# One piece a slot: moving the third batch's first DFT forward, and giving the first expert block its own two PSUM banks

## The chip, the cores and the metric

The program runs on one core of one Trainium2 chip. The metric is device time in microseconds (us), the median of 3 runs. Engines are named as in the profile: PE (TensorE matmuls), PEld (its weight loads), DVE (VectorE), ACT (ScalarE), POOL (GpSimd), SP (SyncE, which issues most DMAs); SPq and ACTq are the DMA-issuing instructions of SP and ACT.

## The reference

`x` has 8 batches of 2496 tokens with 256 features. Step one filters every feature along the tokens in the frequency domain, step two is a mixture of 8 experts with two chosen per token:

```python
X = np.fft.rfft(x, axis=1)
y = np.fft.irfft(X * (filt_r + 1j * filt_i)[None], n=2496, axis=1)
logits = y @ w_gate;  noise_scale = np.log1p(np.exp(y @ w_noise))
top2 = the two largest of logits + noise_scale * noise;  top2_w = softmax over the two
for e in range(8):
    h = np.maximum(y[mask_e] @ w1[e], 0.0)          # 256 -> 1024
    out[mask_e] += top2_w * (h @ w2[e])             # 1024 -> 256
```

## The kernel before

**The filter.** A length of 2496 is 39 x 64. Per batch, 11 pieces of `x` (each 128x512, 256 KB) go through a first DFT of length 39 (`s1`, two-pass fp32 matmul at L338, copy to SBUF by ACT at L381, stored to a scratch tensor `fd` by SP at L382). `kgl` reloads them, `kg1` (L410) does the length-64 DFT and multiplies by the filter (ACT L427 and L428, DVE L429 and L430, POOL L431), `kg2` (L449) the inverse. `logit_sum` (L462), `logits` and `gating` (lg, L491 to L493) give the gate values; `t3` (transposes, L510, ACT L515) and `i2` (L532, ACT L542) end the inverse and write the rows `y` (SP L552). `gate` and `slots` (DVE, with rk at L934, sl at L1005, st at L1030) and `route` (L1072, ra; transposed at L1079) make the list of tokens of each expert, written by POOL (L1091).

**The experts.** A block is 512 token places of one expert. SP reads its list (`lt`, L1109), POOL gathers the rows (L1165). A block of the first batch is turned by POOL (L1237) and PE (xps, L1245); later blocks are turned by DMA transposes (L1204). Weights come by SP (L1291) and are split into two parts by ACT (L1329) and DVE (L1330). The first layer is 8 groups of 6 matmuls (hps, each 128x512; results drained by ACT L1378 and DVE L1379), the second 96 matmuls (yps, each 128x256; drained by ACT L1407, added to `out` by POOL L1408). Two blocks can be filled from the first batch alone; the third needs the list of the second batch.

**The order.** Before the first block, `fft_stream` follows a table: `at(slot, f, ...)` puts a step into a slot, and slots 0 to 31 are issued in order. Batch one runs from slot 0, batch two from slot 14 (its `kg1` in slots 14 to 23, `logit_sum` in slot 26); the third batch's `s1` was put into slots 26 to 31. `pin` makes every engine, SP included, keep the order as written for these steps. The experts, gating and routing are placed between them by the scheduler, from its own estimate of when inputs are ready; the order it settles on is fixed for the chip, and each engine executes its own list strictly in that order. `zero_out` clears rows of `out` (SP L311).

**Banks.** PSUM has 8 banks: hps 2, yps 2, xps 1, fps 3. In the early part `s1` uses the hps banks, and in slots 26 to 31 `t3` and `i2` use the yps banks. A first layer takes hps, hps and a third bank in turn: one of yps for blocks of the first batch (`third`, L1360).

Of the kernel before, what the change touches and what calls it, by code (L numbers as in the profile page):

```python
# [122 lines left out]
def _mm3(nc, o, lh, ll, rh, rl, start=True, stop=True):  # L123
    nc.tensor.matmul(o, lh, rh, start=start, stop=False)  # L124
    nc.tensor.matmul(o, lh, rl, start=False, stop=False)  # L125
    nc.tensor.matmul(o, ll, rh, start=False, stop=stop)  # L126


def f32v(ap):
    return ap.bitcast(F32)  # L130
# [22 lines left out]
class Moe:  # L153
    def __init__(self, ctx, tc, io):
        self.tc, self.nc, self.io = tc, tc.nc, io
        nc = self.nc
        self.cp = ctx.enter_context(tc.tile_pool(name="cp", bufs=1))
        self.dp = ctx.enter_context(tc.tile_pool(name="dp", bufs=1, space=DRAM))
        self.y = self.dp.tile([NROW, YW], I32, name="y")
        self.lst = self.dp.tile([NLR, LR], F32, name="lst")  # L160
        self.wpl = self.dp.tile([E, 2, 4, 128, 1024], F16, name="wpl")
        self.P = ctx.enter_context(tc.tile_pool(name="P", bufs=1))
        self.PS = ctx.enter_context(tc.tile_pool(name="PS", bufs=1, space=PSUM))
        self.xx, self.early, self.last = {}, True, {}
        self.writes, self.reads = [], []
        self.held = self.held_any = False
        self.banks = dict(EARLY)
        self.setup()
        self.tabs, self.wodd = [], 0
        self.sp = self.spw = self.lasta = None  # L170

    def after(self, i):
        return self.tc.issue_after(i.ins) if i is not None else nullcontext()
# [505 lines left out]
    def fft_stream(self):  # L679
# [7 lines left out]
        todo = [(bt, g) for bt in range(NB) for g in range(0, NG, 2)]  # L687
# [33 lines left out]
        def at(slot, g, *a):  # L721
            plan.setdefault(slot, []).append(f(g, *a))
# [22 lines left out]
        at(0, self.load_more)  # L745
        at(0, ahead, 19)
        at(8, self.setup2)
        at(20, ahead, 30)

        for j in range(11):  # L750
            at(7 + j // 2, s1, 11 + j)
# [10 lines left out]
                    at(o, self.t3, *R[i + 1])  # L762
                at(o, self.i2, *R[i])
        for j in range(11):
            at(26 + j // 2, s1, 22 + j)
        at(1, self.init_dram)
        for i in range(4):
            at(18 + i, self.zero_out, 0, i)
            at(24 + i, self.zero_out, 1, i)

        self.pin(self.load_first)
        for j in range(11):
# [568 lines left out]
    def expert(self, parts, may, fill=None):  # L1341

        nc, P = self.nc, self.P
        self.parts, self.ahead, self.standing, self.early_l = parts, [], 0, None
        self.fetch(lambda: True)
        cur = None
        while self.ahead:
            if cur is None:
                cur = self.front(self.ahead[0], fill)
            ent = self.ahead.pop(0)  # L1350
            blk, i = ent[:2]
            lt, n, nt, s, tabi, ready = blk
            w = 128 * nt
            w1, xT, w2st, sc = cur
            if i == 0:
                w2, adds = [], []
            ids, gate = lt[:, i], xT[2]
            if not self.ahead or self.ahead[0][3] or sum(len(a[2][0]) for a in self.ahead) < 4:
                self.fetch(may)
            third = ("xps", 1) if self.by_dma(ent) else ("yps", 2)  # L1360
            hh = []
            for f in range(8):

                tag, bufs = ("hps", 2) if f % 3 < 2 else third
                p = self.PS.tile([128, 512], F32, name="hps", tag=tag, bufs=bufs)[:, :w]
                for kc in range(2):
                    wh, wl = w1[f // 2]
                    o = (f % 2) * 128
                    _mm3(nc, p, wh[:, kc, o:o + 128], wl[:, kc, o:o + 128], *xT[kc], start=(kc == 0), stop=(kc == 1))
                h = P.tile([128, 512], R32, name="hh", bufs=8)  # L1370
                l = P.tile([128, 512], R32, name="hl", bufs=8)
                if ready >= HALF:
                    h, l = hf = h.bitcast(F16)[:, :w], l.bitcast(F16)[:, :w]
                else:
                    h, l = h[:, :w], l[:, :w]
                    hf = f32v(h),
                hold = lambda g: self.pin(g) if self.rows == NB - 1 else g()
                self.relu = hold(lambda: nc.scalar.activation(h, p, AF.Relu))  # L1378
                v = hold(lambda: nc.vector.scalar_tensor_tensor(l, p, 0.0, hf[0], op0=ALU.max, op1=ALU.subtract))  # L1379
                self.resid = v  # L1380
                if f == 4:
                    self.early_l = v
                hh.append((h, l))
                q = (f if f < 4 else None) if n == 1 and nt == 4 else f // 2 if f % 2 else None
                if q is not None and i == 0:
                    w2.append(self.wsplit(w2st[q], "w2", sc))
                yield
            late = not self.ahead
            if late:
                self.fetch(lambda: True)  # L1390
            if self.ahead:
                e2 = self.ahead[0]
                cur = (w1, self.turn(e2), None, sc) if e2[1] else self.front(e2, fill if late else None)
            self.fetch(may)
            yield
            for t in range(nt):


                if t % 2 == 0:
                    bank = self.PS.tile([128, 2, D], F32, name="yps", bufs=2)  # L1400
                p = bank[:, t % 2]
                for f in range(8):
                    h, l = (a[:, t * 128:(t + 1) * 128] for a in hh[f])
                    hl = w2[f // 2][:, :, f % 2]
                    _mm3(nc, p, h, l, hl[:, 0], hl[:, 1], start=(f == 0), stop=(f == 7))
                o = self.slot("yo")
                nc.scalar.activation(o, p, AF.Copy, scale=gate[:, t])  # L1407
                a = nc.gpsimd.indirect_dma_start(  # L1408
                    out=self.io["out"][:BLK + ready * ROWS], out_offset=bass.IndirectOffsetOnAxis(ap=ids[:, t:t + 1], axis=0),
                    in_=o, in_offset=None, compute_op=ALU.add)  # L1410
                for q in adds:
                    self.tc.declare_no_dep(a.ins, q.ins, reason="distinct rows of one expert")
                adds.append(a)
                self.lasta = a
                yield
# [120 lines left out]
```

## Time and profile before

| | us |
|---|---|
| median of 3 runs (2159.06 to 2162.99) | 2160.69 |
| the profiled execution's own time | 2158.89 |
| its span, first to last instruction | 2157.1 |
| PE busy in the span | 2094.6 (97%) |
| DVE, ACT, POOL busy | 1465.0, 1286.0, 1029.5 |
| mean granted TensorE clock, of full speed | 0.993 |

The profiled execution lies 1.80 us under the median. PE is busy nearly throughout, so what can move the end is mostly the time in which PE stands idle, 62.5 us in all.

### The profile page before, as it was taken

To read this page: it belongs to the slowest core of one execution; us is meant where nothing else is said; L and a number is where in the kernel's file an instruction comes from. 1 tells how busy PE (TensorE), PEld (TensorE's weight loads), DVE (VectorE), ACT (ScalarE), POOL (GpSimd) and SP (SyncE) were. 2 spreads that over 40 slices of the span, in tenths; PEclk is the share of its full clock that TensorE was granted. 3 is DMA by queue.
4 is the path that set the end of the run, shared out by engine and by line. 5 is a ranking of instruction groups with operands and counts; after the bars stand their busy time and mean duration, and the time that the engine had idled before them with its cause. 6 is when DMAs were issued, how large, how long until landed. Compare 5 with 4: busy or idle time off the path is not lost.

```text
span 2157.1 us, 42749 instructions
## 1 busy us (share of the span) xinstructions
PE 2094.6 (97%) x14517; PEld 1594.6 (74%) x14517; DVE 1465.0 (68%) x3221; ACT 1286.0 (60%) x2505; POOL 1029.5 (48%) x946
## 2 busy tenths in 40 slices
PE   8779999999999999999999999999999999999997
PEld 6448888888888888766666677666666666667886
DVE  5867778877978886688665976589666664433443
ACT  6766865887577546756565566555556564333443
POOL 4223336334444443445444553556655565654654
PEclk9999999999999999999999999999999999999999
DMA  9688989999999766868676687666989999778997
GB/s 256 186 252 230 228 204 219 228 237 212 230 222 237 172 152 141 199 135 199 150 154 131 148 175 168 145 123 131 238 214 237 231 251 237 169 144 226 273 267 195
DMA packets 511672, 428.47 MB, mean 199 GB/s; under 512 B 215679, under 2 KB 397015, under 8 KB 511447
## 3 DMA queue, kind: packets, MB, share of 16 engines
q1 hardware_dynamic: 440919, 324.49, 56.7%
q0 software_dynamic: 61312, 84.40, 23.2%
q10 hardware_dynamic: 9216, 16.78, 2.8%
q8 instruction: 116, 1.90, 0.4%
q14 instruction: 109, 0.89, 0.1%
HBM read 263.92 MB, written 122.03 MB: 179 GB/s over the span
## 4 chain that ended last, share of the span: by engine, by line
PE 84%; DVE 6%; DMA 3%; ACT 3%; issue 2%; SPq 0%; POOLq 0%; POOL 0%; ACTq 0%; DVEq 0%
PE yps L126 12%; PE yps L124 12%; PE yps L125 12%; PE hps L124 12%; PE hps L125 12%; PE hps L126 12%; PE q L449 3%; PE q L510 1%; DVE hl L1379 1%; PE u L462 1%; DMA stage<-w 1%; PE q L338 1%; PE q L534 1%; PE q L535 1%; PE q L536 1%
## 5 line engine op out<-in xcount | busy, mean ns | idle before, releaser
L1379 DVE SCALAR_TENSOR_TENSOR hl<-hps,hh 128x512 f16<-128x512 f32 (+3 forms) x712 | 434.1, 625 | 371.7 <-ACT hh L1378 304.7
L1408 POOL DMA_INDIRECT out<-stage,ids x316 | 536.8, 1699 | 279.0 <-ACT stage L1407 190.4
L1165 POOL DMA_INDIRECT stage<-y,ids x316 | 341.2, 1080 | 533.7 <-DMA xt<-stage 424.6
L124 PE MATMUL yps<-w,hh 128*128 128x256 f16 (+1 forms) x2048 | 558.0, 278 | 4.3 <-ACT stage L1407 2.7
L125 PE MATMUL yps<-w,hh 128*128 128x256 f16 (+1 forms) x2048 | 553.2, 278 | 0.0
L126 PE MATMUL yps<-w,hl 128*128 128x256 f16 (+1 forms) x2048 | 542.1, 278 | 3.0 <-DVE hl L1379 2.8
L1378 ACT ACTIVATE hh<-hps 128x512 f16<-128x512 f32 (+3 forms) x712 | 376.4, 549 | 196.9 <-PE hps L126 173.6
L125 PE MATMUL hps<-mxl,w1h 128*128 128x512 f16 (+1 forms) x1024 | 394.3, 386 | 1.5 <-DVE mxl L1211 0.8
L126 PE MATMUL hps<-mxh,w1l 128*128 128x512 f16 (+1 forms) x1024 | 392.8, 385 | 0.0
L124 PE MATMUL hps<-mxh,w1h 128*128 128x512 f16 (+1 forms) x1024 | 385.5, 388 | 4.7 <-DVE hl L1379 3.7
L1407 ACT ACTIVATE stage<-yps,gt 128x256 f32<-128x256 f32 x316 | 143.2, 475 | 361.8 <-PE yps L126 180.3
L124 PEld LDWEIGHTS <-hh 128*128 128x128 f16 x1760 | 172.2, 98 | 53.4 <-issue 6.0
L126 PEld LDWEIGHTS <-hl 128*128 128x128 f16 x1760 | 171.4, 98 | 48.7 <-DVE hl L1379 2.0
L125 PEld LDWEIGHTS <-hh 128*128 128x128 f16 x1760 | 172.1, 98 | 32.8 <-issue 1.6
L124 PEld LDWEIGHTS yps<-w,hh 128*128 128x128 f32 x768 | 147.2, 192 | 12.3 <-ACT stage L1407 2.8
L126 PEld LDWEIGHTS yps<-w,hl 128*128 128x128 f32 x768 | 145.9, 192 | 11.5 <-DVE hl L1379 3.4
L125 PEld LDWEIGHTS yps<-w,hh 128*128 128x128 f32 x768 | 146.8, 192 | 6.1 <-issue 1.2
L126 PEld LDWEIGHTS <-w1l 128*128 128x128 f16 x640 | 62.6, 98 | 72.3 <-issue 1.5
L542 ACT COPY yt<-q 117x1024 uint16<-117x1024 uint16 x96 | 91.0, 948 | 41.9 <-PE q L536 21.6
L1235 DVE COPY stage<-xt 128x1024 uint16<-128x1024 uint16 (+2 forms) x174 | 109.6, 683 | 0.9 <-issue 0.9
L125 PEld LDWEIGHTS <-w1h 128*128 128x128 f16 x640 | 62.6, 98 | 52.5 <-issue 3.9
L124 PEld LDWEIGHTS <-w1h 128*128 128x128 f16 x640 | 62.5, 98 | 51.4 <-issue 5.3
(286 smaller groups left out, 4026.3 us busy)
## 6 DMA issues: line engine op xcount, KB each, us to landing
stage<-w SPq DMA_DIRECT2D x328, 256.0 KB
x<-x SPq DMA_DIRECT2D x88, 256.0 KB
fd<-c SPq DMA_DIRECT2D x77, 240.0 KB
fi<-wpl SPq DMA_DIRECT2D x18, 1024.0 KB
fx<-fd SPq DMA_DIRECT2D x140, 128.0 KB
out<-z SPq DMA_DIRECT2D x24, 702.0 KB
wp<-w ACTq DMA_DIRECT2D x64, 256.0 KB
fr<-w SPq DMA_DIRECT2D x16, 1024.0 KB
```

The source lines that it names most:

```text
L124: nc.tensor.matmul(o, lh, rh, start=start, stop=False)
L125: nc.tensor.matmul(o, lh, rl, start=False, stop=False)
L126: nc.tensor.matmul(o, ll, rh, start=False, stop=stop)
L338: nc.tensor.matmul(q, self.rC, x, start=True, stop=True)
L449: nc.tensor.matmul(q3[:, :, 2 * j:2 * j + 2].rearrange("p b r -> p r b"), a[:, j], self.cV, start=True, stop=True)
L542: e = nc.scalar.copy(yt.bitcast(U16)[:, :k, :256].rearrange("p g (two d) -> p g two d", two=2), p.bitcast(U16)[:RP, :2 * m].rearrange("p ( ...
L1165: self.pin(lambda: nc.gpsimd.indirect_dma_start(out=x.bitcast(I32), out_offset=None, in_=self.y[:BLK + ready * ROWS], in_offset=bass.Indir ...
L1235: nc.vector.tensor_copy(xu.rearrange("p (t two) -> p two t", two=2), ent[3][0][:, 2 * kc:2 * kc + 2, :w])
L1378: self.relu = hold(lambda: nc.scalar.activation(h, p, AF.Relu))
L1379: v = hold(lambda: nc.vector.scalar_tensor_tensor(l, p, 0.0, hf[0], op0=ALU.max, op1=ALU.subtract))
L1407: nc.scalar.activation(o, p, AF.Copy, scale=gate[:, t])
L1408: a = nc.gpsimd.indirect_dma_start(out=self.io["out"][:BLK + ready * ROWS], out_offset=bass.IndirectOffsetOnAxis(ap=ids[:, t:t + 1], axis= ...
```

## The change

The third batch's `s1` pieces go from two a slot in slots 26 to 31 to one a slot in slots 18 to 28. Each piece's load is now issued one slot ahead of it; before, eight loads were issued together in slot 20. Four `zero_out` steps go from slots 24 to 27 to slots 28 to 31. The first block's first layer takes its third bank from hps, so that it alternates between two.

```diff
@@ fft_stream
-        at(20, ahead, 30)
         for j in range(11):
-            at(26 + j // 2, s1, 22 + j)
+            at(17 + j, ahead, 23 + j)
+            at(18 + j, self.s1, *todo[22 + j])
         for i in range(4):
             at(18 + i, self.zero_out, 0, i)
-            at(24 + i, self.zero_out, 1, i)
+            at(28 + i, self.zero_out, 1, i)
@@ expert
-            third = ("xps", 1) if self.by_dma(ent) else ("yps", 2)
+            third = ("hps", 2) if self.first else ("xps", 1) if self.by_dma(ent) else ("yps", 2)
+            self.first = False
```

Below, the changed kernel's line numbers are one higher than those of before (L338 is L339, L382 is L383, L1079 is L1080), behind L1360 two higher. Names with numbers are one buffer each.

On SP, from the last row store of the first batch on, before (`x` are loads of the third batch's pieces, `out<-z` are `zero_out`, `tabi` is the table of blocks):

```order
L552 DMA y_60<-yt_1050 117x2x136
L311 DMA out<-z_69 117x12x128 x2
L324 DMA x_1098<-x 128x512
L324 DMA x_1100<-x 128x512
L324 DMA x_1102<-x 128x512
L324 DMA x_1104<-x 128x512
L324 DMA x_1106<-x 128x512
L1107 TENSOR_LOAD tabi_757
```

and now (`c1` is a piece's result, stored to `fd`):

```order
L553 DMA y_60<-yt_1050 117x2x136
L325 DMA x_1054<-x 128x512
L383 DMA fd_1070<-c1_1073 120x2x256
L325 DMA x_1076<-x 128x512
L312 DMA out<-z_69 117x12x128
L383 DMA fd_1070<-c1_1095 120x2x256
L325 DMA x_1098<-x 128x512
L312 DMA out<-z_69 117x12x128
L1108 TENSOR_LOAD tabi_757
```

Each load now stands behind the store of the piece before it, and each store behind that piece's matmul and copy.

On PE, from the second batch's `logit_sum` on, before (u1 and u3 its sums, xps the transposes of a block's rows, lg the gate values):

```order
L462 MATMUL u3_1175<-G_1123,wg_82 32x120
L510 MATMUL q5_1272<-ident_71,G_983 120x128 x4
L479 MATMUL u2_1199<-ident_71,ut0_1192 120x128 x3
L479 MATMUL u2_1205<-ident_71,ut1_1194 120x128
L479 MATMUL u2_1205<-ident_71,ut1_1194 120x96 x2
L510 MATMUL q5_1279<-ident_71,G_983 120x128 x4
L532 MATMUL q6_1286<-tf_1277,cm_85 117x512
L510 MATMUL q5_1291<-ident_71,G_983 120x128 x4
L491 MATMUL lg_1213<-uh_1197,hl_77 117x352
```

and now:

```order
L339 MATMUL q1_1208<-x_1200,cm_85 120x512
L463 MATMUL u1_1215<-G_983,wg_82 32x360 x4
L463 MATMUL u1_1215<-G_1131,wg_82 32x360 x4
L463 MATMUL u3_1216<-G_983,wg_82 32x360 x3
L463 MATMUL u3_1216<-G_983,wg_82 32x120
L463 MATMUL u3_1216<-G_1131,wg_82 32x360 x3
L463 MATMUL u3_1216<-G_1131,wg_82 32x120
L511 MATMUL q5_1313<-ident_71,G_983 120x128 x4
L480 MATMUL u2_1240<-ident_71,ut0_1233 120x128 x3
L1246 MATMUL xps_1749<-ident_71,stage_84 128x128 x4
L480 MATMUL u2_1246<-ident_71,ut1_1235 120x128
```

Eight pieces now stand ahead of the sums, and the first block's transposes ahead of the second batch's gate values.

On PE, at the transpose that ends the second batch's routing (ra_1667), before (yps_2250 and yps_2339 are the second layer of the first block, q1_1811 is a piece of the fourth batch):

```order
L124 MATMUL yps_2339<-w2_1849,hh_1930 128x256
L1079 MATMUL ra_1667<-ident_71,rx_1566 56x128
L346 MATMUL q1_1811<-xh_1807,hl_77 120x512
L347 MATMUL q1_1811<-xh_1807,hl_77 120x512
L348 MATMUL q1_1811<-xl_1808,hl_77 120x512
```

and now (yps_2710 and yps_2793 are the second layer of the second block):

```order
L125 MATMUL yps_2710<-w2_2503,hh_2580 128x256
L126 MATMUL yps_2710<-w2_2503,hl_2581 128x256
L124 MATMUL yps_2793<-w2_2447,hh_2443 128x256
L125 MATMUL yps_2793<-w2_2447,hh_2443 128x256
L126 MATMUL yps_2793<-w2_2447,hl_2444 128x256
L124 MATMUL yps_2793<-w2_2447,hh_2477 128x256
L1080 MATMUL ra_1667<-ident_71,rx_1566 56x128
```

That transpose stood inside the first block's second layer and now stands inside the second block's.

## Rows read from the trace of the kernel before

**Rows 1.** Stages: span, busy us (count) by engine, clock, DMA share, GB/s.

```profile
83.38:108.69 25.31, 17.81 (x124) 12.45 (x123) 25.10 (x78) 12.29 (x23) 10.29 (x7) 1.00 0.68 199
108.69:157.01 48.32, 36.78 (x168) 18.73 (x168) 31.21 (x124) 33.15 (x59) 15.48 (x17) 0.89 0.84 260
157.01:174.19 17.18, 17.18 (x111) 13.95 (x110) 12.46 (x35) 10.07 (x22) 0.00 (x0) 1.00 0.72 214
174.19:216.55 42.36, 38.70 (x233) 34.04 (x231) 29.04 (x52) 30.52 (x63) 20.69 (x20) 0.96 0.93 227
```

**Rows 2.** PE timeline: start, us, operation, count, idle before and releaser.

```profile
108.69 2.76 PE L462 MATMUL u<-G,wg 128*32 128x360 f32 x32
...
132.74 0.60 PE L1245 MATMUL xps<-ident,stage 128*128 128x128 f32 x4
...
157.01 0.79 PE L124 MATMUL hps<-mxh,w1h 128*128 128x512 f32 x1
...
174.19 0.27 PE L1079 MATMUL ra<-ident,rx 128*56 128x128 f32 x1
...
216.55 0.39 PE L124 MATMUL hps<-mxh,w1h 128*128 128x512 f32 x1
```

**Rows 3.** SP timeline, 82 to 135 us: DMA issues.

```profile
85.06 2.32 SPq L311 DMA_DIRECT2D out<-z  x2
87.48 15.28 SPq L324 DMA_DIRECT2D x<-x  x8
...
115.61 1.73 SPq L1109 DMA_DIRECT2D lt<-lst  x2
```

**Rows 4.** A piece: its matmul on PE, its copy on ACT.

```profile
47.40 1.88 PE L338 MATMUL q<-x,cm 117*120 117x512 f32 x4
...
48.46 0.58 ACT L381 COPY c<-q 120x512 f32<-120x512 f32 x1 [0.28 <-PE q L338]
```

**Rows 5.** 256 KB loads: issue on SP, first user on PE; chain of waits.

```profile
1.21 0.89 SPq L324 DMA_DIRECT2D x<-x  x2
...
4.21 7.96 PE L361 MATMUL q<-cm,x 117*128 117x120 f32 x54 [4.21 <-DMA x<-x]
...
202.39 3.93 DMA stage<-w
206.34 0.63 ACT w1h L1329
```

**Rows 6.** POOL timeline: first block's rows turned; second batch's list written.

```profile
128.10 2.35 POOL L1237 COPY stage<-stage 128x1024 uint16<-128x1024 uint16 x2 [4.73 <-DMA stage<-y,ids]
...
177.22 2.28 POOL L1091 DMA_INDIRECT lst<-ro,row  x1 [33.47 <-DVE ro L1088]
```

**Rows 7.** ACT timeline, 95 to 200 us.

```profile
121.00 0.62 ACT L1329 CAST w1h<-stage 128x512 fp32r<-128x512 f32 x1 [1.97 <-DMA stage<-w]
...
133.97 1.28 ACT L912 ACT_TABLE_LOAD   x1
...
150.34 1.01 ACT L542 COPY yt<-q 117x1024 uint16<-117x1024 uint16 x1 [0.58 <-PE q L532]
151.51 0.58 ACT L515 COPY tf<-q 120x512 f32<-120x512 f32 x1
```

**Rows 8.** Waits of PE, whole run: total us, times, longest.

```profile
PE hps L124 <- DVE hl L1379: 4.1, 6, 2.7
```

**Rows 9.** PE timeline, 184 to 236 us: steps of each kind.

```profile
198.29 0.39 PE L124 MATMUL hps<-mxh,w1h 128*128 128x512 f32 x1
...
200.36 0.40 PE L412 MATMUL q<-th,hl 128*128 128x512 f32 x1
...
201.06 0.29 PE L124 MATMUL yps<-w,hh 128*128 128x256 f32 x1
...
202.02 1.05 PE L449 MATMUL q<-cf,a 128*128 128x128 f32 x8
202.83 0.48 PE L412 MATMUL q<-th,hl 128*128 128x512 f32 x1
```

**Rows 10.** Windows after an idle PE (columns as in rows 1).

```profile
120.00:125.00 5.00, 0.21 (x1) 0.00 (x0) 1.67 (x4) 2.34 (x5) 2.76 (x4) 0.88 0.98 293
125.00:130.00 5.00, 4.59 (x9) 2.26 (x10) 4.44 (x10) 3.80 (x6) 1.90 (x2) 0.50 1.00 346
```

More of the change, by code (lines that the diff above doesn't have):

```diff
@@ L170, in __init__ @@
         self.sp = self.spw = self.lasta = None
+        self.first = True
     def after(self, i):
```

## The prediction

> **What bounds the kernel now.** I read the page's first part, then the busy time by stage, then the timelines of PE, SP, ACT and POOL between 80 and 217 us, where the order of work changes. PE is busy 97% of the span, so an edit moves the end only by putting idle PE time in or taking it out. [rows 1] show where the idle time of this part lies: 25.31 - 17.81 = 7.5 us between 83.38 us (slot 18) and 108.69 (`logit_sum` of the second batch), 48.32 - 36.78 = 11.5 from there to the first block's first matmul at 157.01 [rows 2], nothing from there to 174.19 (end of the second batch's routing), and 42.36 - 38.70 = 3.7 up to 216.55, where the third block begins [rows 2]. In slots 18 to 25 DVE is the engine that is full: 25.10 of 25.31 us [rows 1]. From 157 us on PE itself is the bound.
>
> The question is therefore whether 11 pieces can go into the idle time of the first stretch for nothing, and what waits in their stead. A piece takes 0.94 us of PE (two in 1.88 [rows 4]); 8 of them now stand in slots 18 to 25, so at most 8 x 0.94 = 7.5 us of PE work is filled in.
>
> **Step 1, slots 18 to 25.** Before, SP issued the eight loads together at 87.48 [rows 3], and their pieces came 20 us or more later, so no load was waited for. Now SP's order is load, store, load, store. SP executes in order and the store waits for ACT's copy; so the load of piece n+1 is issued only when piece n has been through PE and ACT. One round is: matmul to the start of the copy 48.46 - 47.40 = 1.06, copy 0.58 [rows 4], store and its gap 0.5 (2.32 us for two and 15.28 for eight issues that also wait [rows 3]; 0.45 is what two loads take each, 0.89 / 2 [rows 5]), then the load until PE may read it: 3.0 from 1.21 to 4.21 with little else under way, 3.93 for an equal load of weights under traffic [rows 5]. Sum 1.06 + 0.58 + 0.5 + 3.0 = 5.1, with hand-overs 5.3; with the slower load 6.2. The slots before took (108.69 - 83.38) / 8 = 3.2 us, so the load takes DVE's place as what ends last. PE is in order too, and each piece stands between two slots' `kg1`.
>
> A rule of the Trainium skill bears on this: "DMA: Bandwidth & Descriptors", section "Anatomy of one DMA — SWDGE (gpsimd) path", gives a DMA a fixed 2.0 us and its bytes at 436 GB/s, an estimate of 2.6 us for 256 KB. The trace disagrees, 3.0 to 3.9 us [rows 5]; by the page each round would be 0.4 us shorter and step 1 some 3 us earlier.
>
> The first load takes the place of the `zero_out` at 85.06 [rows 3], lands at 88.1, and the eighth piece starts 7 x 5.3 = 37 us later, at 125; SP also stands at `lt` until 115.61 and issues for 1.73 us [rows 3] between two of these loads, some 2.5 us more. `logit_sum` so begins near 128.5, not 108.69: +20 us. The list of the first batch isn't delayed: its last routing matmuls stand behind the fourth piece, at 88.1 + 3 x 5.3 = 104, near where they ran.
>
> **Step 2, to the first block.** Its rows are turned on POOL from 128.10 for 2.35 us [rows 6], so its xps can't run ahead of 130.5; before they ran at 132.74 [rows 2], now behind `logit_sum` and its copies at about 133. Step 1's delay is hidden for this block up to here. What follows is ACT's list. From the first xps copy to the first matmul's drain it holds 5.5 `yt` copies of 1.01, 6.5 `tf` of 0.58, 8 weight splits of 0.62, 3 piece copies of 0.58, two table loads of 1.28 [rows 4, 7] and about 3 us of small ones: 5.6 + 3.8 + 5.0 + 1.7 + 2.6 + 3 = 21.7, less 0.1 of overlap for each of 30, 18.7. From 133.4 that is 152; PE reaches the first matmul a copy or two sooner, 150.5. Before it was 157.01: -6.5 us. This is the gain: the block no longer waits for all of the second batch's inverse DFT, which is now woven into its first layer.
>
> The bank: with two banks each group of six (1.4 us) must be drained before the next but one. Such waits cost 4.1 us in the whole run of before [rows 8]. Below: 0, since a transpose or an inverse step stands in most gaps; above: 4 us. I take 1, the gaps being filled. Giving the yps bank back gains nothing beyond that start.
>
> **Step 3, the second batch's routing.** Before, 48 hps and 28 yps matmuls stood between the first block's begin and L1079, 17.2 us, all of PE's time [rows 1, 2]. Now there are 96 hps, 118 yps, 6 inverse steps, 14 transposes and 44 routing matmuls there. Steps from [rows 9]: nine hps in 200.36 - 198.29, 0.23 each; three fp32r matmuls of a DFT in 0.70; eight yps in 202.02 - 201.06, 0.12 each; L449 0.81. So 96 x 0.23 = 22.4, 118 x 0.12 = 14.0, and about 11 for the rest (6 x 0.9, 14 x 0.14, 44 x 0.05, small ones): 47 us. L1079 comes at 150.5 + 47 + 1 = 198.5, not at 174.19: +24 us. Noise loads and list reads behind it on SP and POOL follow.
>
> **Step 4, the third block.** It needs the second batch's list. Before, from L1079 it took 3.0 us to the list's write at 177.22 [rows 6], then list, gathers and DMA transposes, then its weights issued at 202.39 and cast from 206.34 for 0.63 [rows 5], with the residual 207.7: 33.5 us after L1079. There it was hidden, since 48 hps and 116 yps were still to do. Now the order leaves 74 yps, 10 triples and 16 matmuls of L449 behind L1079: 74 x 0.12 + 10 x 0.70 + 4 x 0.81 = 19 us, to 217.5. The third block can begin at 198.5 + 33.5 = 232: PE starves for some 14 us. Against 216.55 it is 15.5 later, but then 48 yps more are done (5.7 us): a net 9.7 us late.
>
> The clock: after 5.2 idle us at 120 to 125 the next window ran at 0.50 of full clock, 1.2 instead of 2.4 GHz [rows 10]. A stall of 14 us should end the same way; 5 us at half speed lose 2.5, of which the stall of before has lost some. I add 1.3 (bounds 0 and 3; idle stretches in step 1 included).
>
> **Sum.** 9.7 + 1.3 = +11. Against the profiled execution's 2158.89 that is 2169.9, and with 1.8 us for its distance from the median, 2171.7. The four moved `zero_out` steps I take at nothing: no step waits for what they write there; if their issue stands ahead of a store or a weight load in SP's order, 2.32 / 2 us each [rows 3], it could cost up to 4.6.
>
> **Rivals.**
> - *No starvation (faster).* The 33.5 us of step 4 contain waits of a busy SP and of in-order casts. If the chain takes 19 us or less, PE works through: 150.5 + 47 + 1 + 19 = 217.5, one us after 216.55, with 5.7 more done: -4.7 us, 2156 by the median. It decides from a third block earlier than 222. For: the chain before had no reason to hurry. Against: from the list's write at 177.22 to the weight cast at 206.34 lie 29 us [rows 5, 6], a chain of list write, list read, gathers, transposes and a weight load, one after the other. It could also come from an earlier list of the first batch, as DVE has less to do per us in slots 18 to 22.
> - *About even.* A chain of 24 us puts the third block at 222.5, 6 us after before with 5.7 us more done: 2161.
> - *Loads under traffic (slower still).* With rounds of 6.2 us and the stops at `lt` and weights, `logit_sum` begins at 135 or later, xps after 139; each us then goes through all steps: first block at 156.5, third at 238: +17, 2178. It decides where `logit_sum` passes 129. For: 702 KB of `zero_out` share the queue in the first four rounds. Against: DMA share was only 0.68 in that stretch [rows 1].
> - *The change does nothing there.* If loads of 3 us were hidden, step 1 would vanish, but xps would still hold PE until 130.5, since they now stand ahead of the gate values; steps 2 to 4 would be the same. So this is no separate time.
>
> **How the numbers follow.** Forecast 0.47 (own range 2165 to 2177), loads under traffic 0.19, about even 0.16, no starvation 0.18. 0.2% is 4.3 us, about what a measurement of this kernel can tell from no change. The forecast and the traffic case lie above 2165.0; of the forecast's own spread a little falls below. So slower 0.65, same 0.18, faster 0.17. The range goes from 2155.5 (no starvation) to 2182 (traffic with the clock's upper bound); one case in ten lies outside on each side.
>
> **What would show it.** Step 1: SP's loads of L325 from 85 us on come one every 5 to 6 us, and PE waits for DMA x ahead of L339; rounds of 3.2 us would refute it. Step 2: first hps at 149 to 153. Step 3: L1080 of the second batch at 195 to 203. Step 4: PE idle for 10 us or more before the third block, ended by a weight split or the turned rows, at 228 to 236; a stall under 5 us there makes the forecast wrong, and the time then ends at or below that of before. From there on the stretches should last as before.

## The result and the profile after

The changed kernel takes 2188.86 us (median of 6 runs, 2186.76 to 2194.65), before 2161.07 (6 runs): a ratio of 1.0133 [1.0115, 1.0152], 27.8 us slower. 11 us slower were forecast, with 2182.0 as the upper end. The sign was right; the size was not, and the gain of 6.5 us that was expected at the first block was a loss of 3.8. The profiled execution took 2191.74 us, its span 2189.9, so the two profiled executions stand 32.8 us apart, some 5 more than the medians; the parts below add up to the 32.8.

Where did they arise? Both kernels do the same work, so I cut both traces where PE has done the same amount of it, counting a busy microsecond at half clock as half: after 125, 200, 350 and 1000 us of work. First before, then after; columns as in [rows 1].

```profile
0.00:161.10 161.10, 129.36 (x708) 80.85 (x709) 108.13 (x342) 108.47 (x194) 52.98 (x54) 0.97 0.81 231
161.10:241.50 80.40, 76.74 (x467) 67.06 (x467) 56.58 (x107) 56.67 (x116) 29.46 (x29) 0.98 0.88 225
241.50:400.40 158.90, 152.96 (x992) 134.12 (x991) 126.46 (x294) 109.04 (x227) 68.47 (x52) 0.98 0.93 220
400.40:1054.80 654.40, 650.00 (x4326) 538.40 (x4325) 517.85 (x1129) 435.27 (x850) 287.15 (x241) 1.00 0.83 194
1054.80:2157.10 1102.30, 1085.57 (x8030) 774.22 (x8027) 656.03 (x1352) 576.59 (x1121) 591.47 (x571) 1.00 0.82 192
```

```profile
0.00:173.80 173.80, 138.22 (x691) 87.02 (x692) 99.47 (x293) 107.50 (x192) 51.49 (x54) 0.92 0.73 204
173.80:266.00 92.20, 81.62 (x479) 67.87 (x478) 58.44 (x149) 54.97 (x111) 29.70 (x28) 0.91 0.80 205
266.00:419.70 153.70, 150.00 (x981) 130.32 (x980) 126.03 (x284) 108.82 (x229) 61.81 (x51) 1.00 0.97 223
419.70:1083.10 663.40, 653.43 (x4330) 541.63 (x4329) 522.35 (x1147) 437.06 (x853) 283.18 (x241) 0.99 0.84 193
1083.10:2189.90 1106.80, 1087.34 (x8043) 775.17 (x8040) 657.84 (x1353) 578.38 (x1123) 586.12 (x572) 1.00 0.81 191
```

Take the spans (the number behind each stretch) in pairs: up to and into the first block +12.7 us, over the third block's start +11.8, then -5.2 (a stall of before at 357 to 373 us isn't there), from 400 to 1080 us +9.0, and behind it +4.5.

The first loss. PE's timeline at the pieces (L339), the second batch's `logit_sum` (L463), and the first block's transposes and first matmul:

```profile
90.00 1.47 PE L339 MATMUL q<-x,cm 117*120 117x512 f32 x2 [2.84 <-DMA x<-x]
95.67 1.12 PE L339 MATMUL q<-x,cm 117*120 117x512 f32 x2 [0.19 <-DMA x<-x]
...
112.69 1.12 PE L339 MATMUL q<-x,cm 117*120 117x512 f32 x2 [1.48 <-DMA x<-x]
...
117.81 2.02 PE L339 MATMUL q<-x,cm 117*120 117x512 f32 x2 [2.25 <-DMA x<-x]
...
124.79 2.06 PE L339 MATMUL q<-x,cm 117*120 117x512 f32 x2 [3.30 <-DMA x<-x]
...
131.73 2.03 PE L339 MATMUL q<-x,cm 117*120 117x512 f32 x2 [3.32 <-DMA x<-x]
133.69 3.23 PE L463 MATMUL u<-G,wg 128*32 128x360 f32 x32
...
137.66 0.60 PE L1246 MATMUL xps<-ident,stage 128*128 128x128 f32 x4
...
155.06 0.69 PE L533 MATMUL q<-tf,cm 120*117 120x256 f32 x2 [0.26 <-ACT yt L543]
158.51 1.76 PE L339 MATMUL q<-x,cm 117*120 117x512 f32 x2 [2.75 <-DMA x<-x]
...
160.77 0.78 PE L124 MATMUL hps<-mxh,w1h 128*128 128x512 f32 x1
```

The first eight pieces and the eleventh wait for their loads, 18.5 us in all; the ninth and tenth, which stand further apart, don't. The eleventh stands right ahead of the first block: PE is done with all else at 155.75 and waits until 158.51. SP's timeline shows why the load isn't there: it is issued 0.4 to 0.5 us behind the start of the store of the piece before, every time. Late in the row it also shares SP with the list reads (`lt`) and the block's weights. The last two lines are the eleventh's:

```profile
109.20 0.32 SPq L383 DMA_DIRECT2D fd<-c  x1
109.61 0.38 SPq L325 DMA_DIRECT2D x<-x  x1
110.04 0.40 SPq L312 DMA_DIRECT2D out<-z  x1
114.46 0.32 SPq L383 DMA_DIRECT2D fd<-c  x1
114.87 0.38 SPq L325 DMA_DIRECT2D x<-x  x1
118.36 1.70 SPq L1110 DMA_DIRECT2D lt<-lst  x2
120.25 0.33 SPq L1292 DMA_DIRECT2D stage<-w  x1
120.68 0.41 SPq L383 DMA_DIRECT2D fd<-c  x1
121.19 0.34 SPq L325 DMA_DIRECT2D x<-x  x1
...
154.30 0.39 SPq L383 DMA_DIRECT2D fd<-c  x1
154.78 0.37 SPq L325 DMA_DIRECT2D x<-x  x1
```

From issue to PE the load takes 112.69 - 109.61 = 3.1 us, later 124.79 - 121.19 = 3.6. Behind the longer pauses PE is granted half its clock, and the piece then takes 2.0 us instead of 1.1 (windows of the same trace, columns as above):

```profile
117.90:121.30 3.40, 3.40 (x10) 2.29 (x10) 1.05 (x2) 0.58 (x1) 1.34 (x3) 0.50 0.06 7
121.30:124.70 3.40, 0.18 (x2) 0.00 (x0) 0.00 (x0) 0.58 (x1) 2.68 (x3) 1.00 1.03 266
124.70:128.10 3.40, 3.31 (x9) 2.27 (x10) 0.00 (x0) 0.58 (x1) 1.15 (x2) 0.50 0.91 329
128.10:131.50 3.40, 0.31 (x3) 0.12 (x1) 0.00 (x0) 0.58 (x1) 1.01 (x1) 1.00 0.56 167
```

So PE alternates between waiting and working at 1.2 instead of 2.4 GHz. Of the 12.6 us lost up to 125 us of work, 3.8 are more idle time and 8.9 more work at half clock.

The second loss, in rows of the timeline over several engines: the second batch's routing transpose (PE), its list's write (POOL), the list read (SP), the gathers (POOL), the weights (SP), and the third block's first matmul (PE).

```profile
208.85 0.27 PE L1080 MATMUL ra<-ident,rx 128*56 128x128 f32 x1
...
214.90 1.57 POOL L1092 DMA_INDIRECT lst<-ro,row  x1 [0.31 <-issue]
...
220.50 0.34 SPq L1110 DMA_DIRECT2D lt<-lst  x1
...
223.81 1.04 POOL L1166 DMA_INDIRECT stage<-y,ids  x1 [0.27 <-POOL ids L1116]
...
239.23 1.93 SPq L1292 DMA_DIRECT2D stage<-w  x4
...
242.55 1.22 PE L124 MATMUL hps<-mxh,w1h 128*128 128x512 f32 x2 [4.25 <-ACT w1h L1330]
```

From transpose to block it is 33.7 us, one step after the other, as in before. Whether the weights wait for the list or only for their place in SP's order isn't shown. PE has little more than the 19 us of work that the prediction counted behind the transpose (20.9), waits piecemeal from 223 us on, last for the split of the weights, and works at half clock in between: 8.6 us of idle time and 4.2 lost to the clock.

### The profile page after: what moved, and what is told of

Its sections match the earlier page's. It is cut to its first block, busy times and chain, and to the rows that moved or that the text cites. A ratio compares the mean times of both kernels' runs of the same rounds, so it can differ in the third digit from the quotient of the medians.

```text
span 2189.9 us, 42751 instructions
## 1 busy us (share of the span) xinstructions
PE 2110.6 (96%) x14517; PEld 1602.0 (73%) x14517; DVE 1464.1 (67%) x3221; ACT 1286.7 (59%) x2505; POOL 1012.3 (46%) x946
## 4 chain that ended last, share of the span: by engine, by line
PE 79%; DVE 3%; DMA 2%; issue 2%; ACT 1%; SPq 1%; POOL 0%; ACTq 0%; another core or an unknown queue 0%; POOLq 0%; DVEq 0%
PE yps L124 12%; PE yps L126 12%; PE hps L124 12%; PE yps L125 11%; PE hps L125 11%; PE hps L126 11%; PE q L450 2%; PE q L511 1%; PE u L463 1%; PE q L535 1%; DVE hl L1381 1%; PE q L536 1%; PE q L537 1%; DMA stage<-y,ids 1%; PE q L413 1%
## 5 line engine op out<-in xcount | busy, mean ns | idle before, releaser
L1410 POOL DMA_INDIRECT out<-stage,ids x316 | 527.0, 1668 | 308.7 <-ACT stage L1409 211.3
L124 PEld LDWEIGHTS yps<-w,hh 128*128 128x128 f32 x768 | 146.1, 191 | 15.4 <-ACT hh L1380 2.7
L126 PEld LDWEIGHTS yps<-w,hl 128*128 128x128 f32 x768 | 145.5, 191 | 10.7 <-DVE hl L1381 2.1
L125 PEld LDWEIGHTS <-w1h 128*128 128x128 f16 x640 | 62.6, 98 | 53.6 <-issue 5.5
L1116 POOL CAST ids<-lt 128x4 int32<-128x4 f32 (+3 forms) x66 | 24.8, 376 | 164.3 <-DMA lt<-lst 162.3
```

Of the source, the lines that this page charges most:

```text
L1116: nc.gpsimd.tensor_copy(ids, t)
L1410: a = nc.gpsimd.indirect_dma_start(out=self.io["out"][:BLK + ready * ROWS], out_offset=bass.IndirectOffsetOnAxis(ap=ids[:, t:t + 1], axis= ...
```

## The experiments

Each was timed against before on the same chip (before's own medians were 2158.6 to 2168.0 us), so the ratios are compared. The table gives PE time lost (idle, plus half of the busy time at half clock), worked out from each trace between the same amounts of PE work. Records missing from a trace can shift an entry by 2 us, and two executions of the same order differ by more: PE's order in e9, e13 and e14 is the same up to some 700 us, yet up to 350 us of work they lose 41.6, 45.9 and 44.8 us (before and e12: 50.4 and 53.1). So a difference under 5 us in the first three columns decides nothing. e8, with 13 us more work, and e11 stand in the text.

| | ratio to before | to 125 | 125-200 | 200-350 | 350-1000 | rest |
|---|---|---|---|---|---|---|
| before | 1 | 36.1 | 5.3 | 9.0 | 4.4 | 16.7 |
| changed | 1.0133 [1.0115, 1.0152] | 48.7 | 17.3 | 3.7 | 13.4 | 19.4 |
| e1 load one slot earlier | 1.0052 [1.0033, 1.0071] | 30.6 | 17.7 | 3.1 | 20.8 | 19.6 |
| e2 bank only | 1.0055 [1.0038, 1.0072] | 36.3 | 4.0 | 5.2 | 18.5 | 20.6 |
| e3 no bank edit | 1.0167 [1.0143, 1.0191] | 50.2 | 11.4 | 9.1 | 20.5 | 20.8 |
| e4 load two slots earlier | 1.0004 [0.9983, 1.0024] | 29.8 | 15.2 | 2.3 | 13.8 | 21.0 |
| e5 zero_out only | 1.0012 [0.9998, 1.0027] | 36.5 | 6.0 | 5.1 | 10.6 | 15.0 |
| e6 e4, zero_out back | 1.0052 [1.0034, 1.0071] | 34.9 | 8.5 | 6.6 | 22.7 | 16.5 |
| e7 e4, no bank edit | 1.0084 [1.0067, 1.0101] | 30.5 | 10.5 | 12.5 | 19.9 | 17.4 |
| e9 one a slot from 20 | 1.0016 [1.0, 1.0032] | 32.1 | 7.1 | 2.4 | 20.0 | 18.6 |
| e10 one a slot from 21 | 1.0035 [1.0017, 1.0053] | 37.3 | 4.4 | 6.2 | 12.1 | 19.7 |
| e12 before, pace 170 | 0.9988 [0.9974, 1.0003] | 37.8 | 6.3 | 8.9 | 2.3 | 13.0 |
| e13 e9, pace 170 | 0.9968 [0.9955, 0.998] | 34.7 | 8.4 | 2.8 | 4.8 | 14.6 |
| e14 e9, later pace 125 | 0.9967 [0.9953, 0.9981] | 36.8 | 5.0 | 3.0 | 6.0 | 13.3 |
| e15 changed, pace 170 | 1.0100 [1.0082, 1.0119] | 51.1 | 17.4 | 2.3 | 6.2 | 14.6 |
| e16 e4, pace 170 | 0.9987 [0.9974, 1.0] | 29.5 | 15.7 | 2.3 | 11.0 | 15.4 |

**The loads: e1, e4, e8.** e1 and e4 change one number of the changed kernel:

```diff
-            at(17 + j, ahead, 23 + j)
+            at(16 + j, ahead, 23 + j)      # e1; e4: 15 + j
```

> The changed kernel, but every load of a third-batch piece is issued one slot sooner (two slots ahead of its piece), so that it stands ahead of the store of the piece before; PE's order stays nearly as it was. Theory A (each of the rounds between 85 and 134 us is a load that waits behind a store, 5 to 7 us instead of 3.2, and the short PE pauses in them lower the clock; the late list of the second batch is a second, separate loss): PE waits for DMA x ahead of L339 less than 6 us instead of 18.5, logit_sum of the second batch by 115 instead of 133.7, first hps near 150 instead of 160.8, but PE still pauses before the third block by 8 us or more; time 2170 to 2178 (2188.9 less the 12.6 us of lost PE time up to the first block). Rival B (the loads are all of it): no pause before the third block over 4 us, time 2161 or less. Rival C (the loads are not it, the place of the pieces on PE and the list are): 2183 or more.

> The changed kernel with every load of a third-batch piece two slots sooner (three slots ahead of its piece). Theory A: no wait of PE for DMA x ahead of L339 over 1 us, logit_sum at 108 to 113; with the second batch's routing transpose still behind 96 hps and 121 yps the third block begins with a pause of 8 us or more; time 2168 to 2178, not more than 3 us from one slot sooner. Rival B (loads are all of it): 2161 or less. Rival C: 2183 or more.

PE's wait for x ahead of L339 fell from 18.5 us to 0.5 (e1) and to none (e4). PE of e4, pieces 7 and 8 with `logit_sum` behind them, then the first block, and the third block's start:

```profile
108.06 1.02 PE L339 MATMUL q<-x,cm 117*120 117x512 f32 x2
...
110.46 1.02 PE L339 MATMUL q<-x,cm 117*120 117x512 f32 x2
111.42 2.62 PE L463 MATMUL u<-G,wg 128*32 128x360 f32 x32
...
135.22 0.78 PE L124 MATMUL hps<-mxh,w1h 128*128 128x512 f32 x1
...
190.83 0.27 PE L1080 MATMUL ra<-ident,rx 128*56 128x128 f32 x1
...
223.60 1.22 PE L124 MATMUL hps<-mxh,w1h 128*128 128x512 f32 x2 [3.46 <-ACT w1h L1330]
```

`logit_sum` at 111 instead of 134, the first block at 135 instead of 161, no piece slowed up to `logit_sum`: the rounds were loads behind stores. Theory A holds there, and in the pause of the third block: that block comes 33 us behind the transpose again (e1 33.8, e4 32.8), so the late list is a loss of its own. Two things were missed. The block begins at 133.55 in e1, not near 150. And A's time (2170 to 2178, here 1.0041 to 1.0078) is met by e1 for another reason than A's, by luck: up to 350 us of work e1 is 18.3 us ahead of the changed kernel, not 12.6, and between 350 and 1000 it loses 7.4 of them again. e4 undercuts that time and ends 10 us before e1, where at most 3 were put; 7.0 of this is the 350-1000 column.

e8 tried the clock by itself: matmuls on old data ahead of the pieces that wait.

```diff
+            if bt == 2 and (g0 == 0 or g0 >= 10):
+                for _ in range(2):
+                    nc.tensor.matmul(q, self.rC, f32v(self.hl)[:RP, 0:512], start=True, stop=True)
             nc.tensor.matmul(q, self.rC, x, start=True, stop=True)
```

> The changed kernel with two added matmuls on data long at hand (0.94 us each, their result is overwritten) ahead of the first and of the sixth to eleventh piece's matmul, in the same PSUM bank: PE works while it waits for x. The output does not depend on them. Theory A (of the time lost up to the first block the larger part, 9 of 12.6 us, is the lowered clock that follows each pause of 2 to 3 us, not the pauses): between 85 and 165 us at most three stretches at half clock instead of seven, logit_sum of the second batch at 128 to 132 instead of 133.7 and first hps at 152 to 159 instead of 160.8, in spite of 13 us more PE work. Rival B (the round is the load and SP alone; the clock costs nothing since PE waits anyway): logit_sum at 133 or later, first hps at 160 to 166. The time of the whole tells little, since the second batch's list moves to behind 66 hps and 96 yps and the later order with it: 1.006 to 1.018 of before.

```profile
127.15 2.06 PE L342 MATMUL q<-x,cm 117*120 117x512 f32 x2 [4.23 <-DMA x<-x]
...
134.70 2.62 PE L466 MATMUL u<-G,wg 128*32 128x360 f32 x32
```

Four stretches at half clock instead of seven, but `logit_sum` at 134.70 and the first block at 159.31, with 13 us more PE work done; 1.015 [1.0133, 1.0167]. `logit_sum` came as rival B says; the block came between the two ranges. Filling the waits did not make the load come sooner. But e8 doesn't tell what the clock costs by itself: one of the four stretches was twice as long, some of the added matmuls ran at half clock too, and from the first piece to `logit_sum` PE lost as much to the clock as before the addition (8.1 us, in the changed kernel 7.6). e1 says more: with the loads early, the loss to half clock up to 125 us of work falls from 13.2 to 6.1 us (before: 4.3). So most of it came with the waits.

**The edits one by one: e2, e3, e5, e7.** e2 is before with the two lines of the bank edit, e3 the changed kernel and e7 is e4 without them, e5 is before with `at(28 + i, self.zero_out, 1, i)`.

> The kernel before with the bank edit alone: the first block's first layer takes its third bank from hps. The second batch's routing transpose moves from behind 48 hps and 28 yps to behind 36 hps and 24 yps. Theory A (the bank edit costs only a few waits of two banks for draining): 2161 to 2165, PE hps waiting for DVE hl up to 4 us more than before's 4.1, first hps near 153 or not earlier than before. Rival B (the bank edit lets the first layer start before the inverse DFT and by that makes the list late): 2168 or more. Rival C: it gains 3 us or more.

> The changed kernel without the bank edit (third bank of the first block from yps again); the pieces, loads and zero_out as changed. The second batch's routing transpose stands behind 66 hps and 96 yps instead of 96 and 118. Theory A (load rounds are the first loss and stay, the late list is the second and gets a little smaller): logit_sum of the second batch at 132 to 136 again, time 2180 to 2190. Rival B (the bank edit makes the loss): 2165 or less.

> The kernel before with one edit: the four zero_out steps of the second batch go from slots 24 to 27 to slots 28 to 31; pieces, loads and banks as before. By the order on PE the second batch's routing transpose moves from behind 48 hps and 28 yps to behind 54 and 48, and the later interleaving differs too. Theory A (any edit before 130 us makes the scheduler interleave experts and filter otherwise between 400 and 1080 us, and before's interleaving happened to wait little there): up to 350 us within 4 us of before, PE idle between 400 and 1080 us 8 us or more where before has 4.4, time 1.002 to 1.007 of before. Rival B (the loss between 400 and 1080 us comes from the pieces or the bank): 0.998 to 1.002 of before, idle there under 6 us.

> The changed kernel with loads two slots earlier, without the bank edit. The second batch's routing transpose stands behind 60 hps and 96 yps; 36 hps and 96 yps stand between it and the third block. Theory A: without its own bank the first block waits for an yps bank that the inverse DFT uses, first hps near 135 but the third group of its first layer not before 150; the pause before the third block under 4 us; time 0.997 to 1.006 of before. Rival B (the bank is what lets the block start): first hps at 150 or later and time 1.006 of before or more. Rival C (the bank edit does nothing): within 0.002 of two slots earlier with the bank.

The bank edit alone costs no drain waits (PE hps for DVE hl 3.0 us, before 4.1). Up to 350 us of work e2 loses 45.5 us, before 50.4; by the same mark the bank is worth 1.0 us to the changed kernel and 6.2 to e4, so a gain is likely there but hardly clear of the spread. Yet e2 ends 0.55% slower, a time of rival B without B's reason: the first block began at 157.31 and the list's transpose came at 171.62, 2.6 us before that of before. What it lost stands in its 350-1000 column, which none of its expectations had named as the cause. e3's `logit_sum` came at 134.15 as in theory A; its time is above the range, and PE waited 21.8 us for its loads. e7's block began at 133.65, as theory A says, but its third group at 144.66, not at 150 or later, behind a pause of 3.65 us for DVE that e4 has too (3.47); its time is that of rival B, and why was not shown. e5's time is no change (rival B) with 8.9 us of idle time in the middle (theory A): undecided.

**The list: e6.** e4 with `at(24 + i, self.zero_out, 1, i)` as before, which moves the list forward on PE.

> The changed kernel with loads two slots earlier, and zero_out of the second batch back in slots 24 to 27. On PE the second batch's routing transpose now stands behind 56 hps and 94 yps instead of 96 and 121; 40 hps and 98 yps (some 12 us more PE work) stand between it and the third block. Theory A (the third block starves because the list of the second batch is late on PE): first hps at 134 to 140, the transpose at 176 to 184, the pause before the third block falls from over 8 us to under 4, and at 350 us the run is 5 to 12 us ahead of before; the end depends on 400 to 1080 us, 0.994 to 1.003 of before. Rival B (the pause comes from the weights or from SP and is there wherever the list stands): PE pauses 8 us or more before the third block again.

```profile
182.52 0.27 PE L1080 MATMUL ra<-ident,rx 128*56 128x128 f32 x1
...
221.49 0.48 PE L124 MATMUL hps<-mxh,w1h 128*128 128x512 f32 x1
```

The transpose came at 182.52, the third block at 221.49 without a wait of PE for it, and the loss of that stretch fell from 15.2 to 8.5 us, as theory A says. The other half was missed: the first block began at 144.28, only 0.4 us were gained up to 350, and the middle cost 22.7, 8.1 of them in one wait of a transpose for DVE at 879 us.

**One piece a slot, but later: e9, e10.**

```diff
-            at(18 + j, self.s1, *todo[22 + j])
+            at(20 + j, self.s1, *todo[22 + j])      # e10: 21 + j; loads as in the changed kernel
```

> The changed kernel with the pieces one a slot from slot 20 to 30 and each load three slots ahead (slots 17 to 27); bank edit and zero_out as changed. On PE the second batch's routing transpose stands behind 54 hps and 48 yps, and what stands between it and the third block is 29 us of work, as long as before's 34. Theory A (the loss is the loads behind stores and the late list; the one-a-slot arrangement itself costs nothing): no wait for DMA x ahead of L339 over 1 us, the transpose at 168 to 182, the pause before the third block under 4 us, at 350 us no more lost than before (0 to 6 us less), time 0.994 to 1.003 of before. Rival B (one piece a slot by itself makes slots and drains longer): 1.005 or more, with the loss already there at 160 us.

> As the one from slot 20, with the pieces in slots 21 to 31, each load four slots ahead (slots 17 to 27). The second batch's routing transpose stands behind 51 hps and 42 yps. Theory A: as there, time 0.994 to 1.003 of before and within 0.004 of the one from slot 20. Rival B: 1.005 or more.

e9 has no wait for x, its transpose comes at 174.36 with 29 us of work behind it, and PE never waits for the third block: 8.8 us ahead of before at 350 (e13 and e14, of the same order there, 4.5 and 5.6). One a slot costs nothing by itself. The middle then takes it all back; e10 gains less early and ends a little above its range, by less than its interval.

**The middle: e11 to e16.** PE's order differs from before's up to 1055 us in the changed kernel. A pace table sets how many filter steps are written between expert steps; e12, e13, e15 and e16 change one number (`PACE` 1: 200 to 170), e14 another (`PACES` 115 to 125).

> The changed kernel with loads two slots earlier, and one number of the pace table changed (filter steps per expert step in the second stage, 200 to 240). PE's order is the same up to the second block's second layer, and differs behind it. Theory A (the order between 400 and 1080 us alone moves the time by several us): up to 200 us within 2 us of the run with loads two slots earlier, and the PE time lost between 400 and 1080 us differs from its 13.8 us by 3 us or more; time outside 0.998 to 1.003 of before. Rival B (that order is worth nothing, the 13.8 us are a late effect of the pieces): within 2 us of 13.8.

e11 (e4 with 240) was no test: what moved were buffer numbers, while the order by kind is the same on all engines. It repeats e4: 1.0017 [1.0001, 1.0033], 14.8 us lost in the middle instead of 13.8.

> The kernel before with one number of the pace table changed (filter steps per expert step in the second stage, 200 to 170), nothing else. PE's order is word for word that of before up to 705 us and from 965 us on; between the two the same steps stand in another order. Theory A (which steps stand side by side there is worth several us by itself, and before's order happens to wait little): PE loses 3 us or more over the 2.4 us that before loses between 705 and 965 us, time 1.001 to 1.006 of before. Rival B (that order is worth nothing; the losses behind 400 us follow from what was done earlier): within 2 us there, 0.998 to 1.002.

> The kernel with one piece a slot from slot 20, with the same number of the pace table changed (200 to 170). Same order on PE as that kernel up to some 700 us; it was 8.8 us ahead of before at 350 us of PE work and 2.2 behind at 1000. Theory A (order alone): PE time lost between 700 and 1060 us differs by 3 us or more from its 14.3 us; if it falls to before's 3 us, the time is 0.995 to 0.999 of before. Rival B: within 2 us of 14.3, 1.000 to 1.003.

> The kernel with one piece a slot from slot 20, with the pace of all later stages 115 to 125. Same order on PE as that kernel up to some 800 us, another one from there to some 1800. Theory A (order alone): PE time lost between 800 and 1800 us differs by 3 us or more from the 19.3 us (47.3 to 66.6) that the kernel with pace 115 loses there; time outside 1.000 to 1.003 of before. Rival B: within 2 us of it, 1.000 to 1.003.

> The changed kernel with the number of the pace table at 170 instead of 200. Same order on PE as the changed kernel up to some 720 us, so everything up to there is as lost as it was (24 us more than before by 700 us of PE work). Theory A (what the changed kernel loses behind 720 us is the order there): PE time lost between 700 and 1000 us of work falls from 8.0 to 1 to 4 us, time 1.008 to 1.012 of before. Rival B (it follows from the late start): 8 us again, 1.0115 or more.

> The changed kernel with loads two slots earlier and that number at 170. Theory A: the loss between 500 and 1000 us of PE work, 13.8 us, falls to 3 to 7 us, time 0.993 to 0.998 of before: better than both kernels. Rival B: 13 us again, 0.999 to 1.002.

The stretch from 700 to 1000 us of PE work, first e9 and then e13 (columns as above):

```profile
747.30:1061.60 314.30, 303.33 (x2055) 231.65 (x2054) 239.09 (x560) 185.38 (x341) 141.55 (x121) 0.99 0.71 158
```

```profile
749.30:1050.70 301.40, 299.94 (x2052) 229.88 (x2051) 237.47 (x545) 185.64 (x343) 140.70 (x123) 1.00 0.74 166
```

The same for the changed kernel and e15:

```profile
775.10:1083.10 308.00, 301.73 (x2048) 231.51 (x2047) 239.20 (x560) 184.70 (x341) 140.78 (x122) 0.99 0.72 163
```

```profile
774.60:1077.00 302.40, 299.95 (x2048) 229.75 (x2048) 236.95 (x538) 184.76 (x341) 137.04 (x123) 1.00 0.73 166
```

Same work, same order ahead of it, 12.9 and 5.6 us less. What goes are pauses such as these of e9, ahead of filter steps of a later batch (the profile names no releaser; for the second one e4's names a copy on ACT):

```profile
868.59 0.50 PE L347 MATMUL q<-xh,hl 117*120 117x512 f32 x1 [2.03 <-issue]
...
876.57 0.50 PE L413 MATMUL q<-th,hl 128*128 128x512 f32 x1 [3.12 <-issue]
```

In before the number hardly matters (e12, rival B: 1.1 us lost between 705 and 965 instead of 2.4): its order loses little there with either. e13, e14 and e15 follow theory A, e16 only in part (7.6 us, over the expected 3 to 7, and 0.9987, over A's 0.998). So 12.9 us in e9 and 5.6 in the changed kernel sit in the order of the steps between 700 and 1000 us, which the edits ahead of it had changed. Why a given order waits there was not followed further. e13 and e14 are the versions that beat both kernels, by 0.3% against before. At an equal pace, e13 took 2151.24 us and e12 2156.07 on the same chip (12 runs each): the same edits that end 0.16% above before with 200 (e9, at the edge of its interval) gain 0.2% with 170.

## Why the prediction was wrong

**Step 1, right in kind, 5 us short.** Loads one by one behind stores, PE waiting for x: seen. `logit_sum` came at 133.69 (put: 128.5). The first piece began at 90.00 instead of 88.1, as its load was issued at 86.97, behind a row store, and not at 85.06. The undisturbed rounds are 5.1 to 5.7 us, as the 5.3 put down; but three of the seven take 6.3, 7.0 and 6.9, since the piece runs at half clock behind its pause and the last loads take 3.6 to 3.8 us: 41.7 us for the seven, where 37 and 2.5 for `lt` were put. The stop at `lt` itself held nothing up, for the store behind it, at 120.68, still came 0.2 us behind the end of ACT's copy. The eighth piece, at half clock too, took 2.0 us to `logit_sum` instead of some 0.9. 133.69 is past the 129 at which the text had the traffic rival decide, and short of that rival's 135: rounds of 6.2 us throughout were not seen. The time went beyond the rival's too.

**Step 2 failed.** It said "Step 1's delay is hidden for this block up to here" and took ACT's list as the bound: -6.5 us, the block at 150.5. It came at 160.77, 3.8 later than before. Five of the ten missing microseconds are step 1's: with `logit_sum` at 133.69 the block's xps came at 137.66, not at 133, so the delay was not hidden. The other five are the eleventh piece. The text counted the last three pieces only as copies on ACT; but they too are loads behind stores, and PE is in order, so the eleventh holds the block: 2.75 us of waiting, 1.76 for the piece at half clock, then a group of transposes. ACT's list was not the mistake. PE was done with all but this at 155.75, 22.1 us behind `logit_sum`, where the text has 150.5 - 128.5 = 22; and in e4, where no load is late, the block begins 135.22 - 111.42 = 23.8 us behind it, with PE's pauses on the way ended by ACT's copies. The bank's cost was put at 1 us; in the changed kernel PE's waits of this kind are 3.5 us, not more than in [rows 8]. They are 10.7 us in e4, but 2.9 in e1, whose block starts as early, and 8.5 in e7, without the bank edit: they aren't the bank's.

**Step 3 and step 4, right in length.** 47 + 1 us from block to transpose were put, 208.85 - 160.77 = 48.1 measured; 33.5 us from there to the third block, 33.7 measured. Both only start 10 us late: the third block at 242.55 instead of 232. Of the 14 us of starvation 12.8 came, but 4.2 of them as half clock, so that PE idled for 8.6 us and not for the 10 or more of the sign. By the text's own sum the net is 242.55 - 216.55 - 5.7 = 20.3 us instead of 9.7. By the marks at 200 us of work it is 24.5, since between the third block's start and that mark come another 2.0 us of idle time and 2.5 lost to half clock.

**The clock term was ten times too small.** 1.3 us (bounds 0 and 3) were added; up to that mark the changed kernel loses 13.9 us more than before to work at half clock. Most of this lies inside the lateness of the steps above and is not to be added to it. Up to the first block it came with the waits, as e1 shows; but whoever sums up idle time alone misses it.

**The last sentence failed.** "From there on the stretches should last as before": they give 5.2 back, take 9.0 in the middle and 4.5 behind. e15 shows 5.6 of the 9.0 to be the order there; where the 4.5 come from stays open.

The Trainium skill has the rule that would have spoken against the change: "DMA: Bandwidth & Descriptors", section "Rules for kernel authors", asks to issue a DMA early, compute, and wait late. e1 agrees: one slot earlier takes 18.0 of the 18.5 us of waiting away.

## What to carry to other kernels

A load that is written behind a store on the same issuing engine starts only when that store's data are made; issuing each load one slot sooner was worth 0.8% here. When a stretch is found to be slower, follow every instruction of the moved step to its last one, also where it no longer stands in the stretch. And where a scheduler fills in the rest, time an edit with more than one setting of its pace: an order further on, which the edit doesn't touch, was worth as much as the edit: one number took 12.9 us from that stretch of e9.

## What was not expected of the hardware

Short pauses cost twice: in the changed kernel, behind those of 2.0 to 3.3 us, and once at one of 1.4 (at 101.16), PE was granted half its clock, and a piece that takes 1.1 us took 2.0; behind one of 1.5 us (at 112.69) it was not, nor in before behind one of 2.4 (at 145.81). So where PE is fed by small waits, its work can get dearer too, and the length of a pause alone didn't tell when. And a 256 KB load was ready for PE 2.9 to 3.3 us after its issue in the six pieces before the first block's weights were loaded, and 3.6 and 3.8 us in the two that followed the first of them.
